# When a buffer that GpSimd reads counts as free: a rule of the planner in an attention and SwiGLU kernel

## The chip, the core and the metric

The kernel runs on one core of one Trainium2 chip. The metric is the device time of one launch in microseconds (us), the median of three runs. Engine names are those of the profile: PE is TensorE (PEld its weight loads), DVE is VectorE, ACT is ScalarE, POOL is GpSimd, and SP is the engine that here only issues DMAs. A DMA row of SP (SPq) is the issue of a transfer; the transfer itself lands later.

## What is computed

```python
xn = layernorm(x)                                  # x: 2048 tokens x 512, float32
q, k, v = heads(xn @ wqkv)                         # 32 heads of 16 columns
scores = q k^T / 4, kept where 0 <= i - j < 256    # sliding window of 256 tokens
s = (softmax(scores) @ v) @ wo
f = (silu(xn @ w_gate) * (xn @ w_up)) @ w_down     # hidden width 1792
out = x + s * silu(f)
```

Everything is float32 to the outside. For the dense products each operand is split in a high and a low part (fp32r), and three products stand for one (high by high, high by low, low by high).

## The kernel before

The tokens are cut in four chunks of 512. Dense work goes through PE as a row of units: the q and k projections (tiles `a`), the values (`vp`), gate and up (`g`, `u`), down (`d`) and the output projection (`s`). The contraction is cut in two halves of 64 rows which run side by side on the two halves of PE, so PE takes two 64-row matmuls at a time.

Attention is woven between these. It has 32 units (`u`): four heads by one chunk. For a unit, the kernel (1) loads q and k from DRAM into one of three buffers (`q0` to `q2`, `k0` to `k2`; `load_qk`, eight DMAs); (2) multiplies q and k once to find each row's maximum (tiles `b`, PE; the maximum on DVE); (3) turns the maxima round (`mt`, PE), negates them on ACT into a small tile `ms` and sends `ms` by an 8 KB DMA into two rows of the same q buffer (`q0<-ms0` and so on: the number behind ms is the unit); (4) multiplies k and q again, now with the maximum subtracted (tiles `c`), takes the exponential on ACT (`p`), masks it on POOL; (5) multiplies with the values (`pv`). Step 4 of unit u cannot begin before its `ms` DMA has landed.

A weight comes in four steps: a DMA pair fills one of three raw buffers (`wr`, 128x1024; `raw_take`), ACT rounds it to the high part (`wh`, `w_split`'s `high`), POOL subtracts that from the raw value to get the low part (`wl`, `low`), and PE uses both. `wh` and `wl` live in 16 buffers, freed when PE has passed them. The subtraction on POOL is the last reader of the raw buffer. POOL is also the last reader of a gate tile `h` (the hidden value's low part `hh`), of the reciprocals `r` and of the attention output `o`; these share a ring of fourteen slots (`take`, `give`) with the other short-lived tiles.

All of this order is fixed before the launch by a planner inside the kernel's Python. It keeps a clock, `now`, for the time that it believes has passed, queues of work for DVE, ACT, POOL and the DMA issue (`queue` and `free_at`, under the letters V, S, G, D), and a list of timers (`timer(t, fn, ...)` calls `fn` when the clock reaches `t`). `do` puts an operation in a queue with a believed cost; `pump` emits the operations that are ready. When it emits one, it calls the function that writes the instruction at the operation's believed begin, and `free_at[e]` is then the believed end. The DMA queue is modelled with eight transfers at a time; every transfer on SP waits, on the chip, for the one eight before it. What the planner emits to SP is a strict row: if a DMA waits for its buffer, all DMAs behind it wait too. A weight's fetch is emitted when a raw buffer counts as free (`rfree`).

The order of the dense units is made by `dense_order`, which puts a timed unit in when `work / PACE - LEAD` has reached its due number; the main loop uses the same sum for the attention steps and the marks that start `load_qk`. `LEAD` is in attention units; one unit is `PACE` = 17.6 us of dense work.

The lines at which a buffer is given back inside a POOL operation are 404 and 574 (`raw_give`), 767 (`give(self.h)`), 1265 (`give(box[1])`) and 1273 (`give(box[0])`) of the kernel before.

Of the kernel before, what the change touches and what calls it, by code (L numbers as in the profile page):

```python
# [46 lines left out]
SPARE = 2  # L47
LAG = 7
MW = 80
VDUE = 0.75  # L50


# [1 line left out]
PRIO = -0.5  # L54
MM = 0.2315
PACE = 17.6
LEAD = 1.09
OUT = 2.4
STEP = 0.05
LAND = 3.5  # L60
# [4 lines left out]
def tile_window_attention_swiglu_gate(  # L65
# [47 lines left out]
    free_at = {e: 0.0 for e in "VSGD"}  # L113
# [24 lines left out]
    def timer(t, fn, *a):  # L138
        seq[0] += 1
        heapq.heappush(timers, (t, seq[0], fn, a))  # L140
# [33 lines left out]
    def give(t):  # L174
        slots.append(held.pop(id(t))[1])
# [20 lines left out]
    maskb = pers.tile([P, 3 * P], F32, name="maskb")  # L196
    mts = [pers.tile([P, MW], F32, name=f"m{i}") for i in range(2)]
    qs = [pers.tile([P, 2, TC], F32R, name=f"q{i}") for i in range(3)]
# [128 lines left out]
    def load_first():  # L327
# [66 lines left out]
        def split(raw, j, r, t):  # L394

            def high(a):
                w_take(j, a // 512)
                nc.scalar.activation(wtile[j, a // 512][0][half(r)], raw[half(r), a : a + 512], AF.Copy)

            def low(a):  # L400
                hi, lo = (w[half(r)] for w in wtile[j, a // 512][:2])
                nc.gpsimd.tensor_tensor(lo, raw[half(r), a : a + 512], f32(hi), op=ALU.subtract)
                if r == 0 and a:
                    raw_give(raw)

            def ready(t):
                if (j, r) == (1, 0):
                    low1.append(t)
                else:
                    wready[j, 0] = wready[j, 1] = t  # L410

            for a in (0, 512):
                def done(t, a=a):
                    wpart[j, r, 0, a] = t
                    if a == 0:
                        ready(t)
                    do("G", t, 1.25, lambda: low(a), lambda t: wpart.__setitem__((j, r, 1, a), t), 0.1)

                do("S", t[a // 512], 0.53, lambda a=a: high(a), done, 0.3 + 0.001 * a)
# [100 lines left out]
    def raw_give(t):  # L520
        rfree.append(rtag.pop(id(t))[1])
# [28 lines left out]
    def w_split(j, t, raw):  # L550
        w = [weighted[i].shape[1] if i in weighted else 0 for i in (j, j - 1)]
        both = min(w)
        cuts = [(slice(0, P), a, min(a + 512, both)) for a in range(0, both, 512)]
        if max(w) > both:
            r = 0 if w[0] > both else 1
            cuts += [(half(r), both, max(w))]
        if j not in weighted:
            cuts = [(half(1), 0, 256), (slice(0, P), 256, 512), (slice(0, P), 512, 1024)]
        left = [sum(b <= 512 for _, _, b in cuts), sum(b > 512 for _, _, b in cuts), len(cuts)]

        def high(pr, a, b):
            h = a // 512
            if (j, h) not in wtile:
                w_take(j, h)
                split_next[0] = (j, 1) if h == 0 and max(w) > 512 else (j + 1, 0)
            nc.scalar.activation(wtile[j, h][0][pr, a - 512 * h : b - 512 * h], raw[pr, a:b], AF.Copy)  # L566

        def low(pr, a, b):
            h = a // 512
            hi, lo = (t[pr, a - 512 * h : b - 512 * h] for t in wtile[j, h][:2])  # L570
            nc.gpsimd.tensor_tensor(lo, raw[pr, a:b], f32(hi), op=ALU.subtract)  # L571
            left[2] -= 1
            if left[2] == 0:
                raw_give(raw)

        def done(t, h):
            left[h] -= 1
            if left[h] == 0:
                wready[j, h] = t

        def before(margin, n):
            at = work_at.get(j, total)
            return lambda: now[0] + max(at - work[0], 0.0) * PRESS - margin + 0.3 * n

        spare = now[0] + max(work_at.get(j, total) - work[0], 0.0) - t - 5.0
        t += min(max(0.5 * spare, 0.0), 1.5)
        for n, (pr, a, b) in enumerate(cuts):
            do("S", t, 0.13 + 0.00078 * (b - a), lambda pr=pr, a=a, b=b: high(pr, a, b),
               lambda t, pr=pr, a=a, b=b, n=n: do(
                   "G", t, 0.17 + 0.0021 * (b - a), lambda: low(pr, a, b), lambda t: done(t, a // 512), before(MG, n)),  # L590
               before(MS, n),
               lambda h=a // 512: (j, h) in wtile or (split_next[0] == (j, h) and len(wfree) >= 2))
# [14 lines left out]
    def handover(pb):  # L607
        nc.vector.tensor_copy(pers.tile([MW, 1], F32, name="ho", tag=ring("ho", 2), bufs=1), pb[:MW, 0:1])

# [115 lines left out]
    class GateUp(Stationary):  # L725
# [8 lines left out]
        def done(self, i, pb, t, free):  # L734
            c, fb = self.c, self.fb
            if i == 1 and fb == FB - 1:
                x_used.add(c)
            if i == 0 and fb == (OPEN if c < NCH - 1 else 4):
                o_open.add(c)
                for k in range(KC):  # L740
                    timer(now[0] + 4.0 * k, o_prep, c, k)
            if i == 0:
                def tanh():
                    self.h = take(f"h{c}_{fb}")
                    nc.scalar.activation(self.h, pb, AF.Tanh, scale=0.5)

                def one():
                    nc.vector.scalar_tensor_tensor(self.h, self.h, 1.0, pb, op0=ALU.add, op1=ALU.mult)

                def after_one(t):  # L750
                    free(t)
                    self.ty = t

                do("S", t, 0.5, tanh, lambda t: do("V", t, 0.61, one, after_one, PRIO), PRIO, can=room(1))
                return

            def product():
                nc.vector.scalar_tensor_tensor(self.h, self.h, 0.5, pb, op0=ALU.mult, op1=ALU.mult)
                hid[c, fb] = hidden(f"hh{c}_{fb}")

            def high():
                nc.scalar.activation(hid[c, fb][:, 0, :], self.h, AF.Copy)  # L762

            def low():
                hl = hid[c, fb]
                nc.gpsimd.tensor_tensor(hl[:, 1, :], self.h, f32(hl[:, 0, :]), op=ALU.subtract)  # L766
                give(self.h)

            def after_product(t):
                free(t)  # L770
                do("S", t, 0.52, high, after_high, 1.0)

            def after_high(t):
                do("G", t, 1.24, low, lambda t: hready.__setitem__((c, fb), t), 1.0)

            do("V", t, 0.61, product, after_product, PRIO, can=lambda: self.ty is not None and hfree)
# [473 lines left out]
    def o_prep(c, k):  # L1250
        o_fetch(c, k)
        if (c, k) not in rd_at or len(fetched.get((c, k), ())) < 2 or (c, k) in begun:
            return
        begun.add((c, k))
        hd = slice(8 * k, 8 * k + 8)
        box = fetched[c, k][:1]
        last = c == NCH - 1

        def fetch_r():
            box.append(take(f"r{c}_{k}"))  # L1260
            move(box[1], rd[c, hd, :].unsqueeze(1).to_broadcast([8, DH, TC]))

        def mul():
            nc.gpsimd.tensor_tensor(box[0], box[0], box[1], op=ALU.mult)
            give(box[1])

        def high():
            ot[c, k] = [xn[(c - last) % 2][s][:, k, :] for s in range(2)]
            nc.scalar.activation(ot[c, k][0], box[0], AF.Copy)

        def low():
            nc.gpsimd.tensor_tensor(ot[c, k][1], box[0], f32(ot[c, k][0]), op=ALU.subtract)
            give(box[0])

        def split(t):
            oready[c, k] = t
            if last and (c, 2) in oready and (c, 3) in oready and k >= 2:
                timer(t, rest_low)

        def then_r(t):  # L1280
            do("G", max(t, fetched[c, k][1]), 1.24, mul, then_mul, 1.0)

        def then_mul(t):
            do("S", t, 0.52, high, lambda t: do("G", t, 1.24, low, split, 0.5), 0.5,
               lambda: last or c in x_used)

        dma(max(now[0], rd_at[c, k]), fetch_r, then_r, 0.0, 500, room(1))
# [79 lines left out]
    def max_turn(u, r):  # L1367
# [4 lines left out]
        def go():  # L1372
            nc.tensor.matmul(
                pb[:MW, R * r : R * r + R], mts[u % 2][half(r), :], ident[half(r), half(r)],
                is_transpose=True, start=True, stop=True,
# [246 lines left out]
    def dense_order():  # L1622
        timed = []
        for c in range(NCH):
            for pr in range(NG // 2):
                timed.append((8 * c + 2 * pr - 2.1, Proj(c, pr)))
            timed += [(8 * c + VDUE, WideValues(c))] if c else [(hf - 9.0, Values(hf)) for hf in range(2)]
        timed.sort(key=lambda t: t[0])
# [250 lines left out]
```

## Time and profile before

| | us |
|---|---|
| median of three runs | 852.14 |
| the three runs | 849.75, 852.14, 852.23 |
| the profiled execution | 860.59 |
| its span, first to last instruction | 858.9 |
| PE busy in the span | 845.1 |
| POOL busy | 628.4 |
| DVE busy | 503.1 |
| ACT busy | 490.6 |
| granted TensorE clock, mean | 0.992 of full speed |
| share of the 16 DMA engines, queue of SP | 66.1% |

In this profile a PE row's end is modelled and matmuls overlap, so "busy" rows cover each other; idle time and the granted clock say more. In a table of windows the columns are the stretch, its length, the busy time of each engine with its count of instructions, the granted TensorE clock (PEclk), the DMA engines' busy share and the GB/s moved. In a timeline a row gives start, duration, engine, line, operation, what it writes from what, a count, and in brackets the idle time ahead of it with what ended it.

### The profile page before, as it was taken

To read this page: it belongs to the slowest core of one execution; us is meant where nothing else is said; L and a number is where in the kernel's file an instruction comes from. 1 tells how busy PE (TensorE), PEld (TensorE's weight loads), DVE (VectorE), ACT (ScalarE), POOL (GpSimd) and SP (SyncE) were. 2 spreads that over 40 slices of the span, in tenths; PEclk is the share of its full clock that TensorE was granted. 3 is DMA by queue.
4 is the path that set the end of the run, shared out by engine and by line. 5 is a ranking of instruction groups with operands and counts; after the bars stand their busy time and mean duration, and the time that the engine had idled before them with its cause. 6 is when DMAs were issued, how large, how long until landed. Compare 5 with 4: busy or idle time off the path is not lost.

```text
span 858.9 us, 26300 instructions
## 1 busy us (share of the span) xinstructions
PE 845.1 (98%) x10026; PEld 766.4 (89%) x10026; DVE 503.1 (59%) x1676; ACT 490.6 (57%) x950; POOL 628.4 (73%) x887
## 2 busy tenths in 40 slices
PE   8998999999999999999999999999999999999997
PEld 8998898887998988988888999988898899999887
DVE  4355585564766575666656676565656666554335
ACT  6643746555656447565665546656566664575531
POOL 6755768577759598668696787857697876898871
PEclk9998999999999999999999999999999999999999
DMA  6675856677676895476887686765678768745351
GB/s 171 172 183 131 222 124 166 157 162 170 141 191 160 262 201 122 111 184 147 170 185 158 186 208 188 154 175 118 174 181 196 169 129 203 206 113 134 98 144 52
DMA packets 67142, 139.97 MB, mean 163 GB/s; under 512 B 14710, under 2 KB 17654, under 8 KB 67016
## 3 DMA queue, kind: packets, MB, share of 16 engines
q1 hardware_dynamic: 66552, 137.64, 66.1%
q8 instruction: 79, 1.29, 0.7%
q10 hardware_dynamic: 464, 0.66, 0.3%
q14 instruction: 47, 0.39, 0.2%
HBM read 107.68 MB, written 29.62 MB: 160 GB/s over the span
## 4 chain that ended last, share of the span: by engine, by line
PE 87%; DMA 7%; POOL 3%; SPq 1%; DVE 1%; issue 1%; ACT 0%; DVEq 0%; POOLq 0%; ACTq 0%
PE d L611 17%; PE g L611 16%; PE u L611 16%; PE a L611 10%; PE pv L1535 8%; PE c L1487 6%; PE s L611 5%; PE vp L611 4%; PE b L1339 4%; DMA q<-ms 2%; DMA wr<-wgu 2%; DMA wr<-wdn 1%; SPq L106 1%; DMA o<-od 1%; POOL wl L571 1%
## 5 line engine op out<-in xcount | busy, mean ns | idle before, releaser
L571 POOL TENSOR_TENSOR wl<-wr,wh 128x512 fp32r<-128x512 f32 (+1 forms) x239 | 305.8, 1294 | 79.5 <-ACT wh L566 73.2
L1347 DVE CUSTOM_DVE_ANT_0 jk<-b,maskb 128x384 bf16<-128x384 f32 (+2 forms) x512 | 270.8, 529 | 101.9 <-PE b L1339 58.0
L1447 ACT ACTIVATE p<-c 128x512 f32<-128x512 f32 (+2 forms) x384 | 195.8, 572 | 72.1 <-PE c L1487 67.1
L611 PE MATMUL d<-wh,hh 64*128 64x512 f32 x896 | 232.3, 396 | 0.0
L566 ACT ACTIVATE wh<-wr 128x512 fp32r<-128x512 f32 (+1 forms) x239 | 146.6, 630 | 57.3 <-PE s L611 11.0
L611 PE MATMUL g<-xh,wl 64*128 64x512 f32 x448 | 159.9, 395 | 0.0
L611 PE MATMUL g<-xl,wh 64*128 64x512 f32 x448 | 159.9, 395 | 0.0
L611 PE MATMUL u<-xl,wh 64*128 64x512 f32 x448 | 159.4, 393 | 0.0
L611 PE MATMUL u<-xh,wh 64*128 64x512 f32 x448 | 159.4, 394 | 0.0
L611 PE MATMUL u<-xh,wl 64*128 64x512 f32 x448 | 159.2, 393 | 0.0
L611 PE MATMUL g<-xh,wh 64*128 64x512 f32 x448 | 158.6, 395 | 0.0
L611 PE MATMUL d<-wl,hh 64*128 64x512 f32 x448 | 156.5, 395 | 0.0
L611 PEld LDWEIGHTS d<-wh,hh 64*128 64x128 f32 x896 | 143.2, 187 | 6.6 <-issue 0.2
L1459 POOL TENSOR_SCALAR_AFFINE_SELECT p<-p 128x256 f32<-128x256 f32 x256 | 102.2, 412 | 41.7 <-ACT p L1447 40.2
L766 POOL TENSOR_TENSOR hh<-h,hh 128x512 fp32r<-128x512 f32 x56 | 72.5, 1295 | 52.8 <-ACT hh L762 44.0
L1339 PE MATMUL b<-k,q 48*128 48x384 f32 (+2 forms) x512 | 108.9, 330 | 0.9 <-DMA k<-qkd 0.6
L1487 PE MATMUL c<-q,k 49*128 49x128 f32 (+2 forms) x704 | 95.8, 303 | 5.9 <-DMA q<-ms 5.7
L1463 POOL TENSOR_SCALAR_AFFINE_SELECT p<-p 128x256 f32<-128x256 f32 x224 | 91.2, 413 | 11.3 <-ACT p L1447 10.9
L611 PE MATMUL a<-xh,wl 64*128 64x512 f32 x256 | 97.6, 396 | 0.0
L611 PE MATMUL a<-xl,wh 64*128 64x512 f32 x256 | 97.2, 397 | 0.0
L611 PE MATMUL a<-xh,wh 64*128 64x512 f32 x256 | 96.5, 395 | 0.0
L1487 PEld LDWEIGHTS c<-q,k 49*128 49x128 f32 x704 | 84.2, 188 | 12.7 <-issue 5.6
(118 smaller groups left out, 1935.1 us busy)
## 6 DMA issues: line engine op xcount, KB each, us to landing
wr<-wgu SPq DMA_DIRECT2D x112, 256.0 KB
wr<-wdn SPq DMA_DIRECT2D x48, 256.0 KB
k<-qkd SPq DMA_DIRECT2D x48, 192.0 KB
wr<-wqk SPq DMA_DIRECT2D x32, 256.0 KB
qkd<-qkh SPq DMA_DIRECT2D x32, 256.0 KB
qkd<-qkl SPq DMA_DIRECT2D x32, 256.0 KB
q<-qkd SPq DMA_DIRECT2D x64, 128.0 KB
od<-ev SPq DMA_DIRECT2D x32, 256.0 KB
```

The lines of the kernel that those rows point to most:

```text
L106: eng.dma_start(dst, src)
L566: nc.scalar.activation(wtile[j, h][0][pr, a - 512 * h : b - 512 * h], raw[pr, a:b], AF.Copy)
L571: nc.gpsimd.tensor_tensor(lo, raw[pr, a:b], f32(hi), op=ALU.subtract)
L611: return nc.tensor.matmul(pb, a, b, start=first, stop=last, skip_group_check=True)
L766: nc.gpsimd.tensor_tensor(hl[:, 1, :], self.h, f32(hl[:, 0, :]), op=ALU.subtract)
L1339: nc.tensor.matmul(pb[:, :n], qs[u % 3][r : r + 48, p, qb * P : (qb + 1) * P], ks[u % 3][r : r + 48, p, lo : lo + n], start=True, stop=True,)
L1347: nc.vector.tensor_tensor_reduce(junk[:, :n], pb[:, :n], maskb[:, 3 * P - n :], 1.0, -3.0e38, ALU.add, ALU.max, m[:, col : col + 1],)
L1447: nc.scalar.activation(t[:, h, :], pc[:, :n], AF.Exp, scale=DH ** -0.5)
L1459: nc.gpsimd.affine_select(s, s, [[0, 2], [1, P]], ALU.is_ge, 0.0, base=0, channel_multiplier=-1)
L1463: nc.gpsimd.affine_select(s, s, [[0, 2], [-1, P]], ALU.is_gt, 0.0, base=0, channel_multiplier=1)
L1487: nc.tensor.matmul(pc[:, at0 : at0 + w], ks[u % 3][r : r + 49, p, k0 : k0 + P], qs[u % 3][r : r + 49, p, qb * P : qb * P + w], start=(i == ...
L1535: nc.tensor.matmul(pbs[r][0][32 * j : 32 * j + 32, q0:q1], vt[half(r), (4 * c + kb) % VT, VW * (4 * g + j) : VW * (4 * g + j) + 32], t[hal ...
```

## The change

After the change a buffer whose last reader is a POOL operation goes back to its pool by a timer, at the believed end of that operation plus `SURE` = 0.3 us, where it went back at the operation's believed begin. This holds for the raw weight buffers and for the slots of `h`, `r` and `o`. `LEAD` goes from 1.09 to 1.12. No instruction is added or removed on purpose: the same work is emitted in another order.

```diff
+SURE = 0.3
-LEAD = 1.09
+LEAD = 1.12
...
                 if r == 0 and a:
-                    raw_give(raw)
+                    timer(free_at["G"] + SURE, raw_give, raw)
...
             if left[2] == 0:
-                raw_give(raw)
+                timer(free_at["G"] + SURE, raw_give, raw)
...
                 nc.gpsimd.tensor_tensor(hl[:, 1, :], self.h, f32(hl[:, 0, :]), op=ALU.subtract)
-                give(self.h)
+                timer(free_at["G"] + SURE, give, self.h)
...
             nc.gpsimd.tensor_tensor(box[0], box[0], box[1], op=ALU.mult)
-            give(box[1])
+            timer(free_at["G"] + SURE, give, box[1])
...
             nc.gpsimd.tensor_tensor(ot[c, k][1], box[0], f32(ot[c, k][0]), op=ALU.subtract)
-            give(box[0])
+            timer(free_at["G"] + SURE, give, box[0])
```

What stands where now. On SP, around the first `ms` transfer of the program (unit 0; in a name the number after the letters is the buffer or the unit, the last number a running number of the tile). Before, with the fetches of `wr13` and `wr14` and the first five loads of unit 2 (`q2`, `k2`) already ahead of this piece:

```order
L106 DMA q2_74<-qkd_65 16x2x512
L106 DMA k2_77<-qkd_65 32x2x512
L106 DMA wr15_1180<-wgu 64x1024 x2
L106 DMA k2_77<-qkd_65 16x2x512
L106 DMA q0_72<-ms0_1160 2x8x128
L106 DMA wr16_1256<-wdn 64x1024
```

After, the same place of SP's row:

```order
L107 DMA k2_77<-qkd_65 32x2x512
L107 DMA k2_77<-qkd_65 16x2x512
L107 DMA wr13_1146<-wgu 64x1024
L107 DMA wr13_1146<-wdn 64x512
L107 DMA wr14_1161<-wgu 64x1024 x2
L107 DMA q0_72<-ms0_1174 2x8x128
L107 DMA wr15_1277<-wgu 64x1024 x2
```

All eight loads of unit 2 have moved ahead of the fetches of `wr13` and `wr14`, and `ms0` now stands ahead of the fetch of `wr15` where it stood behind it.

On SP again, around the `ms` transfer of unit 6. Before:

```order
L106 DMA wr32_3373<-wgu 64x1024
L106 DMA wr32_3373<-wqk 64x1024
L106 DMA q2_74<-qkd_65 32x2x512
L106 DMA q2_74<-qkd_65 16x2x512
L106 DMA k2_77<-qkd_65 32x2x768
L106 DMA wr33_3512<-wvk 64x1024
L106 DMA wr33_3512<-wgu 64x1024
L106 DMA k2_77<-qkd_65 16x2x768
L106 DMA q0_72<-ms6_3529 2x8x128
```

After:

```order
L107 DMA wr31_3353<-wqk 64x1024
L107 DMA wr31_3353<-wdn 64x1024
L107 DMA q2_74<-qkd_65 32x2x512
L107 DMA q2_74<-qkd_65 16x2x512
L107 DMA wr32_3540<-wgu 64x1024
L107 DMA wr32_3540<-wqk 64x1024
L107 DMA q0_72<-ms6_3546 2x8x128
L107 DMA k2_77<-qkd_65 32x2x768
```

The `ms` transfer of unit 6 stood behind the fetch of `wr33` and a load of `k2`; it now stands ahead of both, right behind the fetch of `wr32`. The first 24 transfers on SP, and all from the fetch of `wr118` (the last but two of the weights) on, stand as before. Among the 240 dense tiles one pair changes place: `g1_9`, `u1_9` now stand ahead of `a2_0`, `a2_1`.

## The prediction

> **What bounds the kernel now.** I read the busy shares first, then who PE waited for, then the windows and the timeline around those waits, then SP's waits and its row there.
>
> ```profile
> PE   845.1 (98%) x10026; PEld 766.4 (89%) x10026; DVE 503.1 (59%) x1676; ACT 490.6 (57%) x950; POOL 628.4 (73%) x887
> PE c L1487 <- DMA q<-ms: 5.7, 3, 2.7
> PE b L1339 <- DMA k<-qkd: 0.6, 1, 0.6
> SPq L106 <- POOL wl L571: 159.7, 66, 8.1
> 825.39 14.83 PE d L611 x128
> ```
>
> PE is the bound: busy 845.1 of 858.9 us. At its best it takes a 64-row matmul of 512 columns each 14.83 / 128 = 0.116 us (last row, from the chain that ended last), and nothing in this change alters how many there are. So only PE's stalls can be won or lost. In mid program they come from transfers: three waits of the `c` products for an `ms` transfer, 5.7 us in all, and one of `b` for k, 0.6 us. No wait of PE for a weight is in the list. SP, which issues all these transfers in a strict row, stands still 66 times, 159.7 us in all, behind a POOL weight subtraction that still reads the raw buffer into which the next fetch goes. That wait is what the change addresses: the planner emits a fetch at the believed begin of that subtraction.
>
> The two large stalls in the PE timeline, and the clock around them:
>
> ```profile
> 75.38 0.39 PE L611 MATMUL a<-xh,wh 64*128 64x512 f32 x1
> 78.45 0.91 PE L1487 MATMUL c<-q,k 49*128 49x128 f32 x4 [2.68 <-DMA q<-ms]
> 78.00:80.00 2.00, 1.54 (x9) 1.44 (x11) 0.15 (x1) 0.64 (x2) 0.00 (x0) 0.50 0.57 145
> 80.00:82.00 2.00, 2.00 (x14) 1.74 (x12) 0.00 (x0) 0.97 (x2) 1.48 (x4) 0.50 0.00 0
> 82.00:84.00 2.00, 2.00 (x13) 1.94 (x14) 0.15 (x1) 0.60 (x1) 0.88 (x1) 0.50 0.00 0
> 84.00:86.00 2.00, 2.00 (x19) 1.77 (x18) 0.77 (x2) 1.59 (x5) 0.29 (x1) 0.85 0.24 25
> 204.32 0.39 PE L611 MATMUL g<-xh,wl 64*128 64x512 f32 x1
> 206.84 0.56 PE L1487 MATMUL c<-q,k 49*128 49x128 f32 x4 [2.14 <-DMA q<-ms]
> 206.00:208.00 2.00, 1.16 (x12) 1.10 (x12) 0.15 (x1) 0.60 (x2) 0.00 (x0) 0.87 0.60 182
> 208.00:210.00 2.00, 2.00 (x14) 1.82 (x12) 0.35 (x1) 1.88 (x5) 1.36 (x4) 0.50 0.89 241
> 210.00:212.00 2.00, 2.00 (x18) 1.76 (x17) 0.00 (x0) 1.55 (x4) 2.00 (x4) 0.78 0.36 80
> ```
>
> Each stall costs twice: the idle time, and then a granted clock of 0.50 (third number from the end). Stall A (unit 0): 2.68 us idle. In the four windows after it PE was busy 1.54, 2, 2 and 2 us at 0.50, 0.50, 0.50 and 0.85, so 0.77 + 1.0 + 1.0 + 0.30 = 3.07 us of work were lost. A is worth 5.75 us. Stall B (unit 6): 2.14 idle, then 0.13 x 2 + 0.50 x 2 + 0.22 x 2 = 1.70 lost, together 3.84 us. A + B = 9.59 us. The third `ms` stall is what remains of the 5.7 us, 0.88 us, too short for me to charge a clock loss to it.
>
> [...]
>
> **Why the two stalls are there.** ACT writes `ms`, SP sends it, it lands. These are rows of ACT's and SP's timelines and of the chain that ended last:
>
> ```profile
> 66.13 0.27 ACT L1388 ACTIVATE ms<-mt 16x128 fp32r<-16x128 f32 x1 [0.47 <-PE g L611]
> 62.62 1.89 SPq L106 DMA_DIRECT2D wr<-wgu  x2
> 71.76 0.30 SPq L106 DMA_DIRECT2D k<-qkd  x1
> 73.13 1.11 SPq L106 DMA_DIRECT2D wr<-wgu  x2
> 74.97 0.62 SPq L106 DMA_DIRECT2D q<-ms  x1
> 63.20 9.87 DMA wr<-wgu
> 74.97 3.35 DMA q<-ms
> 195.86 0.27 ACT L1388 ACTIVATE ms<-mt 16x128 fp32r<-16x128 f32 x1
> 196.14 0.48 SPq L106 DMA_DIRECT2D wr<-wvk  x1
> 196.66 0.60 SPq L106 DMA_DIRECT2D wr<-wgu  x1
> 199.56 0.61 SPq L106 DMA_DIRECT2D q<-ms  x1
> 199.56 7.15 DMA q<-ms
> ```
>
> A: `ms0` is written by 66.40 and sent at 74.97, 8.6 us later, because the row ahead of it is held at the fetch of `wr15`: that fetch waits for the transfer eight before it, a half of `wr14` that took 9.87 us from 63.20. Then it lands in 3.35 us. B: `ms6` is written by 196.13; the two halves of `wr33` go out ahead of it, and it goes at 199.56 and needs 7.15 us, being behind 512 KB (two 64x1024 float32) and a load of k. So there are two landing times in this trace, 3.35 us and 7.15 us, and I use them as the ends.
>
> **The change part by part.** *Buffers free later.* Five kinds of give-back move by the believed cost of the POOL operation plus 0.3 us. The row for the price on the chip:
>
> ```profile
> L571 POOL TENSOR_TENSOR wl<-wr,wh 128x512 fp32r<-128x512 f32 (+1 forms) x239 | 305.8, 1294 | 79.5 <-ACT wh L566 73.2
> ```
>
> One subtraction is 1.294 us, so a fetch is emitted about 1.6 us later. On SP that by itself costs nothing: the chip's fetch never could start before POOL's end, and the average wait of 159.7 / 66 = 2.4 us shrinks by up to 1.6. What is won is what now stands ahead of the fetch instead of behind it. No operation is added; POOL, ACT and DVE do the same work.
>
> *Stall A.* Now wr12's fetch is followed by the eight loads of unit 2, then `wr13`, `wr14` and `ms0`. The loads carry 4 x (128 + 64) = 768 KB (32x2x512 and 16x2x512 float32), `wr13` 256 + 128, `wr14` 512: 1664 KB. The DMA engines in this stretch moved (last column):
>
> ```profile
> 60.00:64.00 4.00, 4.00 (x39) 4.00 (x38) 3.64 (x14) 1.16 (x2) 0.47 (x2) 1.00 0.70 199
> 64.00:68.00 4.00, 4.00 (x40) 3.81 (x38) 2.49 (x13) 1.52 (x4) 3.39 (x3) 1.00 0.91 225
> 68.00:72.00 4.00, 4.00 (x41) 4.00 (x39) 3.57 (x14) 2.08 (x4) 1.73 (x2) 1.00 0.82 115
> 72.00:76.00 4.00, 3.78 (x35) 3.33 (x31) 3.60 (x14) 0.93 (x3) 3.31 (x3) 1.00 0.69 193
> ```
>
> Their mean is 183 GB/s: 1664 KB are 9.1 us. Before, `wr14` went out at 62.62, with `wr13` (384 KB, 2.1 us) just ahead of it; the eight loads take its place from about 60 on, so the bytes ahead of `ms0` are through at about 69. `ms0` itself is written later: its `mt` stands 16 dense matmuls further on in PE's order, 16 x 0.116 = 1.9 us, so at 68.3. It lands, by the two ends, 3.35 to 7.15 us after, at 71.7 to 75.5. PE reaches `c` of unit 0 after 74 dense matmuls behind `mt`, where it had 72; before, it stood there at 75.8 (75.38 + 0.39), so now at 75.8 + 1.9 + 0.2 = 77.9. Room: 2.4 to 6 us. I take A as gone. It stays, at the other bound, if `wr13` or `wr14` waits out SP's longest POOL wait, 8.1 us, just there.
>
> *Stall B.* `ms6` now stands behind `wr32` (out at 191.16 to 194.0 before) and ahead of `wr33`. Written at 196.13, it can go at once; landing 199.5 to 203.3. PE came to `c` at 204.7 (204.32 + 0.39); now 60 dense matmuls instead of 52 stand between `mt` and `c`, so 205.6. Room: 2.3 to 6 us; I take B as gone.
>
> *What is given back.* The whole middle of SP's row is shuffled, and the planner draws the `c` products nearer to `mt`: in PE's order the dense matmuls between them go from 104 to 64 in unit 2, 87 to 53 in unit 11, 69 to 44 in unit 12, 68 to 38 in unit 29; over all 32 units the mean goes from 59 to 54. Two large stalls in 32 units is the rate of the old row. With SP's waits shorter by up to 1.6 us of 2.4, I charge one stall of the size of B, 3.84 us; bounds are none and three of the mean size (9.59 / 2 = 4.8), 14.4.
>
> *LEAD.* 0.03 x 17.6 = 0.53 us of dense work, by which attention steps fall due later. Its direct price at the end is the `pv` of unit 31 five dense matmuls later, 0.6 us fewer of dense tail, with no idle either way: nothing. It is part of the shuffle.
>
> **The sum.** The profiled execution took 860.59 us (span 858.9): 860.59 - 9.59 + 3.84 = 854.84. The timed median is 852.14, 8.45 below the profiled execution; I do not know whether the stalls are as long there, and carry the difference over unchanged: **846.4 us**, a gain of 0.7%.
>
> **Rivals.** *The near products stall (slower).* Take unit 29:
>
> ```profile
> 735.26 0.27 ACT L1388 ACTIVATE ms<-mt 16x128 fp32r<-16x128 f32 x1
> 737.45 0.59 SPq L106 DMA_DIRECT2D q<-ms  x1
> 746.40 0.45 PE L1487 MATMUL c<-q,k 49*128 49x128 f32 x3
> ```
>
> `ms29` went 1.9 us after it was written and PE came 9.0 us after that. With 30 dense matmuls fewer, 3.5 us, only 5.5 are left, and in the new row the pair of `wr105` still stands right ahead of `ms29`. A landing of 3.35 us fits, one of 7.15 stalls PE 1.7 us and halves the clock behind. The point from which it decides is a landing over 5.5 us. If that happens in three of the shortened units at 4.8 us each while A and B go: 852.14 - 9.59 + 14.4 = 857.0. For it: landing is slow just behind a pair of weights, as in B. Against: the planner shortened these distances because it believes less stands ahead, and after the change its belief about fetches is nearer to the chip. Chance 0.20.
>
> *Weights come late (slower).* Each fetch is 1.6 us later and q and k loads cut in ahead. In POOL's and PE's orders the nearest subtraction past the start stands 48 dense matmuls ahead of its use, 5.6 us, in both; the median falls from 185 to 174, 21.5 to 20.2 us. It decides if PE's list shows weights or `wl` as releaser. At eight places of 1.6 us, with A and B gone, it gives 852.14 - 9.59 + 12.8 = 855.4. Nothing in PE's waits speaks for it. Chance 0.08. [...]
>
> *One for one (the same).* A and B go and two others come, or they are shorter in the timed runs than in the profiled one, as the 8.45 us between them could mean; or the fetches wait for raw buffers whose subtraction is late anyway, SP's 159.7 us stay, and the change only redraws the lots. 852.14, give or take 2.5. Chance 0.17.
>
> **How the numbers follow.** Forecast 0.55, same 0.17, slower 0.20 + 0.08 = 0.28. About 0.3%, 2.6 us, is what a measurement of this kernel can tell from no change; the forecast's own range, 841 to 849.5, lies beyond it. The low end is everything gone: 852.14 - 9.59 - 0.88 - 0.6 = 841. The high end is the first rival, 857.
>
> **What would show it.** Right: no `q<-ms` wait of PE over 1 us at 78 and 206 us, a granted clock of 1.00 there, SP's wait for `wl` well below 159.7 us. Wrong: PE waits on `q<-ms` of 5 us or more in other units with 0.50 clocks behind them (first rival), PE waiting on ACT or POOL weight tiles (second), or a time unchanged although A and B are gone from the trace (third).

## The result, and the profile after

The change made the kernel faster by half a percent: 849.50 us (median of 21 runs, 848.98 to 856.25) against 853.23 us (21 runs, 849.75 to 859.69), ratio 0.9951 with a 95% interval of 0.9935 to 0.9968. The median moved by 3.7 us, the fastest run by only 0.8. What changed most is the distance from the fastest run to the median: 3.5 us before, 0.5 us after.

The profiled execution of the changed kernel is the slowest of its 21 (856.25 us, span 854.5), and must be read with that in mind. Who PE waited for in it, and the first rows of SP's waits (line numbers are one higher than before):

```profile
PE xp L450 <- DVE xt L352: 1.7, 1, 1.7
PE warm L250 <- DVE warm L245: 1.1, 1, 1.1
PE s L612 <- DVE ho L609: 0.4, 1, 0.4
```

```profile
SPq L107 <- POOL wl L572: 118.0, 51, 9.6
SPq L107 <- DVE m L1348: 36.6, 27, 5.4
SPq L107 <- DVE ho L609: 31.8, 11, 14.4
```

There is no wait of PE for a transfer left: the three `q<-ms` waits (5.7 us) and the wait for k (0.6 us) are gone. SP stands behind the `wl` subtraction 51 times for 118.0 us, where it was 66 times for 159.7. Its waits for other things grew (behind DVE's `m` from 19.1 us to 36.6, behind `ho` from 24.5 to 31.8); no wait of PE came of that in this profile.

The 159.7 us are a total over the whole program, and they don't lie where the two large stalls came from. These are SP's waits in the kernel before, first from 58 to 76 us (unit 0, the whole list), then from 186 to 201 us (unit 6, the first four of ten rows):

```profile
SPq L106 <- DMA wr<-wgu: 4.7, 3, 2.0
SPq L106 <- DMA qkd<-qkl: 0.7, 1, 0.7
SPq L106 <- DVE m L1347: 0.5, 1, 0.5
SPq L106 <- DMA wr<-wdn: 0.3, 1, 0.3
```

```profile
SPq L106 <- POOL p L1463: 1.4, 1, 1.4
SPq L106 <- DMA wr<-wgu: 1.0, 1, 1.0
SPq L106 <- DMA qkd<-qkl: 0.9, 1, 0.9
SPq L106 <- POOL p L1459: 0.8, 1, 0.8
```

No row names `wl`, and none of the other six of the second list does. What held `ms0` were weight transfers that stood ahead of it in the row and had not landed (three waits, 4.7 us); what held `ms6`, once it was written, were two landings as well (0.9 and 1.0 us) and the issues ahead of it. So at these places it is the order of SP's row that counts, that is, what the planner put ahead of `ms`, and not a wait for POOL.

Why the profiled execution of the changed kernel is slow shows in the windows of its first 28 us:

```profile
8.00:12.00 4.00, 3.45 (x19) 3.17 (x19) 3.86 (x11) 2.95 (x5) 2.12 (x3) 0.73 0.65 161
12.00:16.00 4.00, 4.00 (x16) 2.99 (x16) 1.12 (x4) 1.45 (x4) 2.01 (x2) 0.50 0.88 205
16.00:20.00 4.00, 4.00 (x21) 4.00 (x21) 2.60 (x12) 2.54 (x5) 2.92 (x3) 0.50 0.02 4
20.00:24.00 4.00, 4.00 (x44) 4.00 (x44) 0.15 (x1) 2.56 (x4) 2.08 (x2) 0.56 0.65 158
24.00:28.00 4.00, 4.00 (x77) 4.00 (x77) 0.60 (x3) 1.70 (x6) 0.00 (x0) 1.00 0.36 104
```

Behind the 1.7 us gap at the first rows' transposes the granted clock stays near 0.50 for some 15 us: 3.45 x 0.27 + 4 x (0.50 + 0.50 + 0.44) = 6.7 us of PE's time. Without it the execution would stand at 849.5, where the other twenty are (848.98 to 849.94). This is no effect of the change: the profile of a kernel further down that keeps the old give-back (`ms` on ACT's queue) has the same start, with 0.82, 0.50, 0.50, 0.50 and 0.97 in these five windows.

The two places of the old stalls, in the timelines of ACT, SP and PE. First unit 0, then unit 6:

```profile
74.63 0.27 ACT L1389 ACTIVATE ms<-mt 16x128 fp32r<-16x128 f32 x1 [2.21 <-PE b L1340]
75.64 1.10 SPq L107 DMA_DIRECT2D wr<-wgu  x2
76.84 0.61 SPq L107 DMA_DIRECT2D q<-ms  x1
79.93 1.13 SPq L107 DMA_DIRECT2D wr<-wgu  x2
84.42 0.59 PE L1488 MATMUL c<-q,k 49*128 49x128 f32 x4
```

```profile
197.11 0.27 ACT L1389 ACTIVATE ms<-mt 16x128 fp32r<-16x128 f32 x1
197.81 0.60 SPq L107 DMA_DIRECT2D wr<-wqk  x1
198.51 0.61 SPq L107 DMA_DIRECT2D q<-ms  x1
206.72 0.45 PE L1488 MATMUL c<-q,k 49*128 49x128 f32 x4
```

`ms0` goes out 1.9 us after it is written (8.6 before), and the fetch of `wr15`, which stood ahead of it, goes 3.1 us behind it. `ms6` goes out 1.1 us after it is written (3.4 before). PE comes to `c` 7.6 and 8.2 us after the issues and does not wait.

### The profile page after: what moved, and what is told of

Same layout as the page of the kernel before. It is cut to its first block, busy times and chain, and to the rows that moved or that the text cites. A ratio compares the mean times of both kernels' runs of the same rounds, so it can differ in the third digit from the quotient of the medians.

```text
span 854.5 us, 26324 instructions
## 1 busy us (share of the span) xinstructions
PE 846.9 (99%) x10026; PEld 759.8 (89%) x10026; DVE 503.0 (59%) x1676; ACT 489.5 (57%) x950; POOL 627.8 (73%) x887
## 4 chain that ended last, share of the span: by engine, by line
PE 98%; DMA 1%; DVE 0%; issue 0%; ACTq 0%; DVEq 0%
PE u L612 19%; PE d L612 19%; PE g L612 19%; PE a L612 11%; PE pv L1536 8%; PE vp L612 6%; PE c L1488 6%; PE s L612 5%; PE b L1340 4%; PE xp L632 1%; DMA xt<-x 1%; PE xp L450 0%; DVE xt L352 0%; DVE s L1189 0%; DVE st L347 0%
## 5 line engine op out<-in xcount | busy, mean ns | idle before, releaser
L612 PE MATMUL d<-wh,hh 64*128 64x512 f32 x896 | 227.6, 393 | 0.0
L612 PE MATMUL d<-wl,hh 64*128 64x512 f32 x448 | 152.7, 394 | 0.0
L612 PEld LDWEIGHTS d<-wh,hh 64*128 64x128 f32 x896 | 140.5, 185 | 6.7
L1488 PE MATMUL c<-q,k 49*128 49x128 f32 (+2 forms) x704 | 97.6, 299 | 0.0
L612 PE MATMUL a<-xl,wh 64*128 64x512 f32 x256 | 92.9, 392 | 0.0
L612 PE MATMUL a<-xh,wl 64*128 64x512 f32 x256 | 92.7, 392 | 0.0
L612 PE MATMUL a<-xh,wh 64*128 64x512 f32 x256 | 92.3, 392 | 0.0
```

The source lines that it names most:

```text
L612: return nc.tensor.matmul(pb, a, b, start=first, stop=last, skip_group_check=True)
L1488: nc.tensor.matmul(pc[:, at0 : at0 + w], ks[u % 3][r : r + 49, p, k0 : k0 + P], qs[u % 3][r : r + 49, p, qb * P : qb * P + w], start=(i == ...
```

## The experiments

Theory 1: a fetch emitted at the believed begin of the POOL subtraction holds SP's row on the chip; an `ms`, q or k transfer behind it lands late and PE stalls. Its rivals: the change is a lucky redraw of the order, by `LEAD` as much as by the give-back; or the landings are slow for another reason. The waits shown above already speak against one link of theory 1: at the two large stalls SP was not behind that subtraction. What the experiments can still tell is whether the time of the give-back, by the order that it makes, brings the stalls. All ratios below are to the kernel before, run on the same chip at the same time.

### The two parts apart

The late give-back with `LEAD` left as it was:

```diff
+SURE = 0.3
 LEAD = 1.09
```

> The late give-back alone, LEAD left at 1.09. Theory 1 (the row of SP is held by fetches emitted too early, ms transfers stand behind them, PE stalls): no wait of PE for an ms transfer over 1 us in the profile, SP's wait behind the wl subtraction well under 159.7 us, the runs within 1 us of each other as after the change, ratio to before about 0.995. Rival (the change only redraws the order; this draw was a lucky one, made by LEAD as much as by the give-back): ms waits of 2 to 6 us are there again, ratio 1.000 or above, runs spread over several us.

And `LEAD` alone:

```diff
-LEAD = 1.09
+LEAD = 1.12
```

> LEAD 1.12 alone, buffers given back at the begin as before. Theory 1: SP's wait behind the wl subtraction stays near 160 us, ms waits of PE of 2 us and more somewhere, runs spread over several us, ratio 0.998 to 1.005. Rival (a lucky draw by LEAD): ratio about 0.995, no ms waits.

| | median us (runs) | fastest | ratio | SP behind wl |
|---|---|---|---|---|
| late give-back, 1.09 | 847.48 (6) | 846.79 | 0.9939 [0.9915, 0.9963] | 93.8 |
| old give-back, 1.12 | 853.56 (12) | 850.57 | 1.0015 [0.9992, 1.0039] | 155.5 |

The late give-back brings the whole gain, and `LEAD` 1.12 brings none; beside the late give-back it stands 2 us higher than 1.09 (849.50 against 847.48; the two were not run side by side, and the intervals of their ratios overlap). The runs of the late give-back alone lie 2.4 us apart, where I expected 1. In the profile of `LEAD` alone the stall of unit 0 is still there, and the windows behind it have something to say on its price:

```profile
78.00 0.56 PE L1487 MATMUL c<-q,k 49*128 49x128 f32 x4 [2.41 <-DMA q<-ms]
76.00:78.00 2.00, 0.01 (x2) 0.04 (x2) 0.69 (x4) 0.31 (x1) 1.26 (x1) 1.00 1.04 212
78.00:80.00 2.00, 2.00 (x20) 1.93 (x22) 0.15 (x1) 1.44 (x3) 0.28 (x1) 1.00 0.41 92
80.00:82.00 2.00, 2.00 (x22) 1.97 (x21) 0.87 (x3) 1.42 (x5) 2.00 (x4) 1.00 0.00 0
```

PE stood for 2.41 us and the clock stayed at 1.00: here the stall cost its idle time, and no loss of clock shows behind it.

### Which buffers

The raw weight buffers alone (`LEAD` 1.12):

```diff
-                raw_give(raw)
+                timer(free_at["G"] + SURE, raw_give, raw)
```

> LEAD 1.12 and the late give-back for the three raw weight buffers alone; the slots of h, r and o are given back at the begin as before. Theory 1: all of the gain, ratio about 0.995, no ms waits, since the held fetches are those into raw buffers. Rival (the slots matter as much): ms or other transfer waits of PE of 2 us and more, ratio 0.998 or above.

The slots of `h`, `r` and `o` alone (`LEAD` 1.12):

```diff
-                give(self.h)
+                timer(free_at["G"] + SURE, give, self.h)
...
-            give(box[1])
+            timer(free_at["G"] + SURE, give, box[1])
...
-            give(box[0])
+            timer(free_at["G"] + SURE, give, box[0])
```

> LEAD 1.12 and the late give-back for the slots of h, r and o alone; the raw weight buffers are given back at the begin as before. Theory 1 (held fetches into raw buffers are the cause): nothing gained, ratio 0.998 to 1.004, SP's wait behind wl near 160 us, runs spread over 5 us and more. Rival (any later give-back loosens the plan): ratio about 0.996, runs within 1 to 2 us of each other.

| | median us (runs) | fastest | ratio | SP behind wl |
|---|---|---|---|---|
| raw buffers | 848.93 (9) | 847.99 | 0.9955 [0.9937, 0.9974] | 116.7 |
| slots | 852.83 (12) | 850.85 | 0.9990 [0.9966, 1.0013] | 153.2 |

The raw buffers carry it. The slots' runs lie 4.5 us apart, a little less than expected, and with the slots alone PE still waits for transfers, at 56 and 79 us:

```profile
PE b L1340 <- DMA k<-qkd: 2.4, 1, 2.4
PE c L1488 <- DMA q<-ms: 1.3, 1, 1.3
```

### Is it luck of the draw?

`LEAD` 1.06, once with the old and once with the late give-back:

> A third draw of the order with the old give-back: LEAD 1.06. Theory 1: SP's wait behind wl 150 to 165 us as in the other old draws, PE waits of 1 to 3 us for an ms, q or k transfer somewhere, median 2 us or more above the fastest run, ratio 0.997 to 1.004. Rival (luck of the draw): any of these may be missing; a median within 1 us of the fastest run with the old give-back would speak against theory 1.

> A third draw with the late give-back: LEAD 1.06. Theory 1: SP's wait behind wl 90 to 120 us, no PE wait for a transfer over 1 us, median within 1 us of the fastest run, ratio 0.992 to 0.996. Rival (luck of the draw): PE waits of 2 us and more, ratio 0.998 or above.

And the raw buffers alone at 1.09:

> The late give-back for the raw weight buffers alone, LEAD 1.09: the smallest form of the change. Theory 1: the whole gain, ratio 0.993 to 0.996, no PE wait for a transfer over 1 us; if the slots' late give-back costs or gives anything it shows as a difference of over 1 us to the 847.5 to 848.1 us of the two kernels with all five give-backs late at this LEAD.

| | median us (runs) | fastest | ratio | SP behind wl |
|---|---|---|---|---|
| old give-back, 1.06 | 852.61 (12) | 849.63 | 0.9976 [0.9950, 1.0003] | 137.0 |
| late give-back, 1.06 | 848.83 (12) | 847.76 | 0.9951 [0.9927, 0.9976] | 106.9 |
| raw buffers late, 1.09 | 847.50 (10) | 847.26 | 0.9912 [0.9881, 0.9942] | 94.6 |

SP's wait in the old draw at 1.06 was lower than I expected (137.0 for 150 to 165), but the rest held: its profile has a PE wait of 1.9 us for `ms` at 77 us, the late one has none for a transfer (its median stands 1.1 us above its fastest run, where I expected at most 1). At each `LEAD` the old order's median stands 3 to 4 us above its fastest run and the late order's 0.5 to 1.1. I read this as a floor that each order has of its own, with stalls on top where the give-back is early. The fastest runs differ too: 849.6 to 850.6 us for the three old orders, 846.8 to 849.0 for the three late ones.

The traces say more against luck than the times. In all four kernels with the early give-back of the raw buffers (before, `LEAD` 1.12, `LEAD` 1.06, the slots alone), `ms0` stands behind the fetch of `wr15` and goes out 7.2 to 8.6 us after it is written. In all seven with the late one it stands ahead of that fetch and goes out 0 to 2.2 us after, and no wait of PE for a transfer is in their lists.

The last row equals the 847.48 of all five give-backs late: at this `LEAD` the slots bring nothing that shows, and raw buffers alone at 1.09, within 0.6 us in all ten runs, lie below both kernels of this study. Its ratio is below what I expected (0.993 to 0.996) because the kernel before came out slower beside it (853.91).

### How late

Nothing on top of the believed end, and a further 1.3 us on top, both at `LEAD` 1.09:

```diff
-SURE = 0.3
+SURE = 0.0    # the second: 1.3
```

> All give-backs at the believed end of the POOL operation with nothing on top (SURE 0), LEAD 1.09. Theory 1: the 1.3 us of the operation itself is the part that counts; ratio 0.993 to 0.996 as with 0.3, runs close together. Rival (only lateness with slack on top helps): between before and after, ratio 0.997 to 1.000, runs spread over several us.

> All give-backs 1.3 us after the believed end, LEAD 1.09. Theory 1: SP's wait behind wl falls further, below the 93.8 us at 0.3, and the time stays within 0.2% of that (ratio 0.992 to 0.996), since no ms wait is left to remove; later fetches have cover (the nearest weight is 5.6 us ahead of its use). Rival (weights come late): PE waits for weights or their splits, ratio 0.998 or above.

Measured: 848.10 us, ratio 0.9937 [0.9916, 0.9957], SP behind `wl` 118.6 us; and 848.80 us, ratio 0.9939 [0.9919, 0.9959], 73.1 us. The end of the operation is what counts; the 0.3 us on top adds nothing that shows. At 1.3 us SP's wait falls by a further 20.7 us and no time comes of it: PE no longer waits for a transfer, and SP's total wait behind `wl` is not what costs. Weights do not come late either: no wait of PE names one.

### Other roads to the same end

If the place of `ms` in SP's row were all, taking the `ms` transfers out of that row should do as well:

```diff
-            move(qs[u % 3][48 : 113 : 64], box[0])
+            move(qs[u % 3][48 : 113 : 64], box[0], nc.scalar)
```

> The kernel before, with the 32 ms transfers issued from ACT's own DMA queue, so that they never stand behind a held fetch on SP; everything else stays. Theory 1: no ms waits of PE, the two stalls with their half clock gone, ratio about 0.995 (849.5 us), minus or plus what 32 issues cost on ACT (each about 0.6 us of its sequencer, off the path). Rival (the stalls come from slow landings on full DMA engines, not from the place in the row): the stall of unit 6 stays near 2 us, ratio 0.998 or more.

It did not: 853.87 us, ratio 1.0012 [0.9987, 1.0037], runs from 849.20 to 860.74. The number is the rival's, but its mechanism is not there: the `ms` waits are gone from the profile, that of unit 6 too. Another wait stands in their place. From PE's timeline and the chain that ended last (start, duration, what):

```profile
83.14 0.91 PE L1339 MATMUL b<-k,q 48*128 48x384 f32 x2 [1.95 <-DVE m L1347]
70.80 6.99 DMA wr<-wgu
77.85 2.96 DMA wr<-wgu
80.87 0.61 ACT wh L566
81.48 0.49 ACT h L745
82.00 0.69 DVE h L748
82.75 0.33 DVE jk L1347
83.14 0.44 PE b L1339
```

Read downwards: the fetch of a weight goes out late (77.85, when an earlier one has landed at 77.79) and lands at 80.81; ACT's split of that weight begins at 80.87; then come a tanh on ACT (`h`, 81.48), a step of DVE (82.00) and the maximum (`jk`, 82.75), and at 83.14 PE begins the `b` product for which it stood 1.95 us. The fetch need not have been all that held ACT: its timeline is idle for 5.21 us up to 80.33, and in that gap `ms0` goes out on ACT's own queue (79.16, an issue of 1.13 us), 6.1 us after it was written. What that issue waited for is not shown. So by this chain a late fetch reached PE through ACT's row, where before it did so through SP's, and closing the first road left the second open. My theory 1 named only the first. The second accounts for at most 1.95 us in the one trace, with the clock at 1.00 behind it. The same trace lost 6.7 us to the halved clock at the start, ahead of any `ms`. The timed runs show less clock too: the mean granted clock is 0.9957 over the twelve, against 0.9983 for the kernel before beside them, which is 2.2 us of the span. Why these runs lose more clock, and so why they lie as high as before's, is not shown.

The last one leaves the give-back alone and lets the planner believe every transfer's landing 1.5 us later:

```diff
-GUARD = 1.5
+GUARD = 3.0
```

> The kernel before with the planner's allowance on every transfer's landing raised from 1.5 to 3.0 us (GUARD); buffers are given back at the begin as before. Theory 2, a wider form of 1 (what costs is that the plan believes transfers sooner than the chip has them, whoever holds the row; ACT and PE then stand in order behind a late one): most of the gain comes by this road too, ratio 0.994 to 0.997 and runs close together, though SP still waits near 160 us behind wl. Theory 1 in its narrow form (the held row itself must go): ratio 0.998 to 1.003.

853.90 us, ratio 1.0003 [0.9981, 1.0025]: the number of the narrow theory 1, not the gain that theory 2 expected, and yet the runs lie within 0.94 us of each other (853.45 to 854.39), and no PE wait names a transfer, while SP stands behind `wl` for 155.4 us. So the held row need not go for the stalls to go: here too `ms0` stands ahead of the next fetch and goes out 1.5 us after it is written. Padding every landing takes the stalls away as well, but the order that comes of it has a floor some 4 us higher. Where the 4 us lie is open: PE is busy 844.5 us in its profile against 838.5 in that of the late give-back at 1.09, with the same 10026 matmuls and a granted clock of 1.00 in both in every 100 us up to 800, so it is not idle time; how PE's matmuls follow one another is where I would look.

## Why the prediction was right, point by point

**What bounds it.** Right: only PE's stalls could move. One step was wrong: I took SP's 159.7 us behind the `wl` subtraction for the wait that the change addresses. Neither large stall has that wait behind it (SP's waits around units 0 and 6), it fell by 20.7 us more without a gain when the give-back came 1.3 us after the believed end, and it stayed at 155.4 us where the landings were padded and no stall was left. The sentence that carried the forecast was the other one, that what is won is what now stands ahead of the fetch instead of behind it.

**Stalls A and B.** Both gone, and by the order, as forecast. The estimate for unit 0 was `ms0` written at 68.3 and PE at `c` at 77.9; less the 6.7 us of that execution's slow start the trace has 68.2 and 77.7. For unit 6 the trace has 190.7 and 200.0 by the same subtraction, over 5 us ahead of the estimate (196.13 and 205.6), which left out that everything comes sooner once A is gone; the room is the same. That the row was held at the fetch of `wr15` was only the last part of it: SP waited for landings at two loads of unit 2 (1.7 and 2.0 us) before it waited at that fetch (1.0).

**Their price.** The term of the sum that was too large. I took 9.59 us from one execution and carried the 8.45 us between it and the timed median over unchanged. That execution, 860.59 us, lies above all 21 timed runs of the kernel before, and half of the 9.59 is a halved clock that a stall need not bring: 2.41 us of standing still brought none when `LEAD` alone was changed. What the stalls are worth in the timed runs can only be estimated. The distance of the median from the fastest run gives 3.5 us, if the fastest run has none of them; the four kernels with a late give-back at `LEAD` 1.09 gain 5.3 to 6.4 us by their medians. Of that gain the recorded clocks give the halved clock 0.8 to 1.7 us (the span times what the mean clock lacks of 1, the kernel before less the late one, without two executions of the kernel before, 863.29 and 866.08 us), where the sum had 4.77. The third rival had named this, that the stalls might be shorter in the timed runs, but drew no change of the forecast from it. Two slips in the working change nothing: 1664 KB of 1024 bytes take 9.3 us at 183 GB/s, not 9.1, and in the first window behind stall B PE was busy for 1.16 us, not 2, which makes B 3.73 us.

**What is given back.** Charged at one stall of 3.84 us; no new stall is in the trace. If the stalls were worth what `LEAD` 1.09 gains, the draw at 1.12 gave back some 2 us as a higher floor, which the sum did not have. The forecast gain was 5.7 us (0.7%), the measured one 3.7 (0.5%), and 849.50 lies on the upper edge of the forecast's own range, 841 to 849.5. That it came so near is partly luck: a price too high by 3 to 6 us and a charge too high by about 4 mostly cancelled.

**LEAD.** Put down as nothing by itself, and 1.0015 with 1.000 inside the interval agrees. As part of the shuffle it may not be nothing: beside the late give-back it stands 2 us above 1.09, in kernels not run side by side.

**The rivals.** The near products did not stall: no wait for `ms` is left, in unit 29 or elsewhere. Weights did not come late, even with the give-back a further 1 us later. The redraw of lots is real in size, some 2 us between floors, but four kernels with the early give-back of the raw buffers had stalls and seven with the late one had not.

## What to carry to other kernels

Where a planner fixes the order of a strict queue, let a buffer count as free when its last reader ends. Counted free at the reader's begin, it put its next transfer too far ahead in SP's row here, and the price was paid by a small transfer that had nothing to do with that buffer and stood behind: `ms0` went out 8.6 us after it was written, and 1.9 after the change. Look for it at each stall: which small transfer came late, how long after its data was written it went out, and what stood ahead of it. A queue's long total wait for one reader is no measure of it: here that total moved without the time (93.8 to 73.1 us), and the stalls went without it (at 155.4). Moving the small transfers to another queue took their waits away here and left PE a stall of 1.95 us behind ACT and DVE. And price a stall from many timed runs, not from one profiled execution.

## What I had not expected of the hardware

A short stall on PE did not cost the same each time. Gaps of 2.68 and 2.14 us were followed by a halved granted clock for about 6 and 4 us in the profile of before, and one of 1.90 us with the old give-back at `LEAD` 1.06 by some 4 us of a lowered one:

```profile
76.00:78.00 2.00, 0.79 (x8) 0.80 (x10) 0.48 (x2) 0.30 (x2) 1.26 (x1) 1.00 0.80 183
78.00:80.00 2.00, 2.00 (x15) 1.90 (x14) 0.15 (x1) 1.37 (x3) 1.07 (x3) 0.60 0.04 10
80.00:82.00 2.00, 2.00 (x14) 1.98 (x13) 0.15 (x1) 0.60 (x1) 1.30 (x2) 0.54 0.00 0
```

Gaps of 2.41 us (`LEAD` alone), 2.38 us (the slots alone) and 1.95 us (`ms` on ACT's queue) had a granted clock of 1.00 behind them. At the start, gaps of 1.7 and 1.5 us ahead of the transposes were followed by some 15 us near 0.50 in two profiles (after the change, and `ms` on ACT's queue), and one of 1.2 us in the profile of before by 1.00 throughout. So the length of the gap does not tell the two cases apart: 1.90 us with a loss, 2.41 without. What does is not shown by these traces.
